# Attention tiles turned by TensorE in place of DMA, the last two score banks read by one exponential, and two units' bias moved from TensorE to a table

## The chip, the cores and the metric

The kernel runs on one core of one Trainium2 chip. The metric is the device time of one execution in microseconds. A core has five engines that each take their instructions in order and wait for one another through semaphores: TensorE (PE in the profile, its weight loads PEld), VectorE (DVE), ScalarE (ACT), GpSimd (POOL) and SyncE (SP). SP and POOL issue most of the DMAs.

## What is computed

Attention with a sliding window of 128 and a linear bias (ALiBi) for 8 batches of 8 heads, 576 positions and 64 dimensions; its output, seen as 4608 tokens of 512 features, goes through two matrix products with an ELU between them.

```python
scores = q @ k.T / sqrt(D)
mask = (rel >= 0) & (rel < 128)          # rel = query position - key position
scores = where(mask, scores - slope[head] * abs(rel), -1e9)
attn = softmax(scores)
x = (attn @ v).transpose(0, 2, 1, 3).reshape(4608, 512)
h = x @ w_in                             # w_in 512 x 2048
g = where(h > 0, h, exp(min(h, 0)) - 1)
out = g @ w_out                          # w_out 2048 x 512
```

## The kernel before

**Tiles.** Keys go in units u of 128 (u = 0 to 3; the last also takes the 64 keys left over). For each batch b and unit u the scores of all heads, keys on partitions, stand in four PSUM banks of 512 columns, `sp[0]` to `sp[3]`: two heads of 256 queries in each. `sp[0]` and `sp[1]` are the halves of one tile `spa`; `sp[2]` and `sp[3]` are tiles of their own. ScalarE takes the exponential into `EX[u]` (fp16), VectorE multiplies by a table `TAB` of exp(bias) with zeros outside the window, and a product with v, widened by a column of ones, gives a tile `xn` of 128 queries (64 in the fifth, i = 4) by 512 features, divided by that column's sum. The tile is turned, features to partitions, into a ring `xT`. From it come hidden blocks of 512 columns in the banks `hp[0]` and `hp[1]` by turns, then a relu or exponential on ScalarE, a second exponential on ScalarE or a minimum on GpSimd, and the ELU's end on VectorE (`g`). Output tiles of 256 tokens are formed by seven products of half-size matrices (Winograd's form of Strassen's scheme), `product`, from sums S1 to S4 of `g` and T1 to T4 of `w_out`.

**Batches 0 and 1.** They have functions of their own, since they run while the weights are still loading. For batch 0, units 0 and 1 in two calls each (`early_bias`, `early_scores`) and units 2 and 3 (`bias`, `first_scores`) put the bias into PSUM by a product of `SI` (identity times slope) with `RB` (distances, with a large negative number outside the window), and the scores are added to it. `RB` has 512 columns, the second 256 in the order of unit 3. Batch 1 is weighted by the table instead (`first_weigh`).

**Turning.** The nine tiles of batch 0 and of batch 1's first four are turned by TensorE (`turn_x`, L295: four transposes of 128 columns into a PSUM bank; L297: a copy to `xT` on ScalarE or VectorE). The other 31 tiles are turned by a DMA from SP's queue (`turn`, L287).

**Order.** The order is written out by hand in `SCRIPT`. Each token takes the next job from the queue of its name, and its instructions go to their engines in that order; a semaphore is waited for only where data or a buffer require it. The tokens that matter here:

- `f`, `fA`, `fD`: q and k of batches 0 and 1 turned by TensorE, and copied by ScalarE or VectorE; `b` bias; `i` scores of batches 0 and 1; `j` their exponentials; `W` `first_weigh`; `C` four copies that fill the second halves of `RB` and `TAB`
- `k` scores of a unit from batch 2 on (L222, 32 partitions an operand, four at a time); `x`, `y`, `z` exponentials of `spa`, `sp[2]`, `sp[3]` (L230, L233); `w` weighting of half a unit (L238)
- `v` product with v (L250, L271), `r` reciprocal, `n` division into `xn`; `T` the DMA transpose; `t`, then `tA` or `tD`: `turn_x` and its copy
- `h` a hidden block (L312), `p` and `q` its two steps to `e` (L319 to L325), `e` the ELU (L333)
- `oN` N steps of products (L403), one matmul of 256 columns each; `u` the copy of a finished product, `s1` to `s4` sums, `c1` to `c4` and `m` results and their stores; `O` outputs of the first 256 tokens
- `l` loads of `w_out`, q, k and v on POOL's queue; `d` q and k turned in blocks by VectorE

The first loads (k, q, v and the four quarters of `w_in`, L119) are issued by POOL ahead of `SCRIPT`.

Of the kernel before, what the change touches and what calls it, by code (L numbers as in the profile page):

```python
# [7 lines left out]
F32 = mybir.dt.float32  # L8
# [10 lines left out]
def kernel(  # L19
# [38 lines left out]
    RB = fore[3][:, 1024:1536]  # L58
# [18 lines left out]
    sp = [spa[:, 0, :], spa[:, 1, :]] + [ps_s.tile([128, 512], F32, name=f"sp{i}", tag=f"sp{i}") for i in (2, 3)]  # L77
# [72 lines left out]
    with tc.manual_schedule():  # L150
# [11 lines left out]
        def bias(u, half, d):  # L162
            r0 = 256 * int(u == 3)
            for x in (2 * half, 2 * half + 1):
                for hh in range(2):
                    c = 256 * (x % 2)
                    nc.tensor.matmul(pairs[d][hh][:, c:c + 256], SI[:, 4 * hh + x, :], RB[:, r0:r0 + 256],
                                     start=x % 2 == 0, stop=False, skip_group_check=True)

        def first_scores(b, u, half, d):  # L170

            heads = [(x, hh) for x in (2 * half, 2 * half + 1) for hh in range(2)]
            for o, kb, q0, n in blocks(u):
                for x, hh in heads:
                    r, c = slice(64 * hh, 64 * hh + 64), 256 * (x % 2) + o
                    k0 = x * S + 128 * kb
                    nc.tensor.matmul(pairs[d][hh][:, c:c + n], kt_[b][r, k0:k0 + 128], Q0[b][r, x, q0:q0 + n],
                                     start=b > 0, stop=True, skip_group_check=True)
# [48 lines left out]
        def expo(b, u, g):  # L227
            if g < 2:
                if g == 0:
                    nc.scalar.activation(unit(b, u)[:, 0:2, :, :], spa.rearrange("p g (h c) -> p g h c", h=2),  # L230
                                         AF.Exp, scale=0.125)
                return
            nc.scalar.activation(unit(b, u)[:, g, :, :], sp[g].rearrange("p (h c) -> p h c", h=2),  # L233
                                 AF.Exp, scale=0.125)
# [48 lines left out]
        def turn(b, i):  # L283
            n = 128 if i < 4 else 64
            o = (b * S + 128 * i) % RING
            x = xnt.pop((b, i)).rearrange("p g h d -> p (g h d)")
            nc.sync.dma_start_transpose(out=xT[:, :, o:o + n], in_=x[0:n, :])  # L287

        def turn_x(b, i, copy, bank):
            n = 128 if i < 4 else 64  # L290
            o = (b * S + 128 * i) % RING
            x = xnt.pop((b, i)).rearrange("p g h d -> p (g h d)")
            t = bank.bitcast(F16)[:, 0:512].rearrange("p (c r) -> p c r", c=4)
# [187 lines left out]
        V.scalar_tensor_tensor(out=RB[:, 0:256], in0=rel, scalar=-1.0, in1=far, op0=ALU.mult, op1=ALU.add)  # L481
# [5 lines left out]
        for h in range(H):  # L487
            nc.scalar.activation(TAB[:, 0, h // 2, h % 2, :], RB[:, 0:256], AF.Exp, scale=slope[h])
# [31 lines left out]
        for b in range(2, B):  # L520
# [19 lines left out]
            f fD f fD b f fA f fD C C C C b i j i j j b i j j v r n v r n b t tD v r n v r n  # L540
            h p q t tD f fA
            e h p q i j f fD f fA f fD b b i j i l
            h p q e j j l
            h p q e b i l
            h p q j v r n v r n e l
            h p q t tD b i j e l
            h p q e
            h p q e
            h p q e v r n v r n
            h p q e l O  # L550
            h p q e v r n t tA l
            h p q e a v r n l l l O
            h p q e a t tA
            h p q e a l O
            h p q e a l O O1 O2
            h p q e a l O
            h p q e a f fD f fA l l O
            h p q e a f fA f fD f fA f fA l l O
            e a l l s1 s3 O O1 O2 i j i j j
            W l l o7  # L560
            s2 W l l o1 u o6 v r n i j i j j
            l l o2 c1 o5 v r n
            W W d l o3 u o4 t tA i j v r n
            W l s4 o4 u o3 v r n
            h p q v r n i j d l
            h p q e W t tA d l o5 u o2
            h p q e v r n i j l
            h p q e W t tA l o7 c2
            h p q e v r n i j d l
            h p q e W l o7 u  # L570
            h p q e v r n v r n l c3 m s1
            o1 h o2 p o1 k l q o1 e o1 v y l t tA d o1
            h x r n e o1 T o1 p o4 s2 u
            h q w o2 e o2 z o4 d p o1
            h w q c1 o2 p v e o4 q o1 r
            h s3 u n o2 p o2 e o1 T o1 u k s4 q o1
            h x e d o2 p o3
            h w u q y l o1 z e o4 p o2 d o1
            h d q w l o1 e v p o2 c2 l o1 q o1
            h r n l o1 e o1 T p o2 l o2 s1 o1 q k l u o1 e o1 x  # L580
            h l d o2 p o1 s2 o4 u
            h w q y e o4 z o2 c3 o2 p o2 w m
            h q c1 v u e p o4 s3 o1 q o1
            h r n o2 p o1 e o1 T o1 k q s4 u
            h e x d o3 p o2 w o1
            h y q z l o1 e o1 u o3 p o1 w o2
            h q d l o1 v c2 p e o1 l o2 q o2 r o2 v l u e v o2
            h r l s1 n o2 p o2
            h r T n q n o2 p e k u d o1 q o3
            h x s2 e o2 p o3 w o3 q o1  # L590
            h c1 y e o1 z o2 s3 o2 p o3 w o1
            h u q c3 v m e T o3 u o2 r o1 p s4 o3
            h n q o1 e T o1 p k d u q
            h x l e o2 p o1 w o4 z o1 q
            h c2 y l e o2 p o2 w l o4 q
            h s1 l e o1 v l p o2 r o1 q l
            h n u d o2 p k e q o3 s2 o2 u
            h x e s3 o2 p o3
            h w q c1 y o1 e o4 z o2 c3 o2 p o1 s4
            h m T u w q o4 e v u p o2 r o3 n o1 q o1  # L600
            h T e o3 u k p c3 q
            h x l e o2 p o2 w o3 y o1 q
            h c2 z l e o2 p o2 w l o2
            h q s1 l v e p l o2 r o1 u v d q o1 m l o1
            h e o1 n o1 p o4 v r T q s2 o3
            h u e o1 s3 o1 p o2
            h r n q c1 o2 n p o3 e o1 T o2 q k d u
            h x e s4 o2 p o1
            h w z d q o5 u o2 e o1 p o4 y o2 q o1
            h u w o1 e o1 p o3 v c3  # L610
            h q r n l o2 e p o1 T o2 l o2 s3 q k l u c2
            h x e m l o3 p
            h w l q s1 l o2 z o2 e o3 y o5 p o1 w
            h q s2 v u e p o4 c1 o1 q
            h r n o2 e p o1 T o4 u s4 k q
            h x e d o2 p o3
            h w u q o1 y o1 e o4 p o2 d o1
            h z q u w l o2 p o3 e o2 v q
            h l r e o1 l n o1 p o5 s3 l T q k c2 u l e
            h x l o2 p o1 w o1  # L620
            h l q s1 o1 z o1 e o4 y o2 c3 o2 p
            h w m q s2 o1 v u p o1 v r o1 e o2 q o1 v c1 o3 e o1
            h u n o2 r p o1 T o1 n
            h r q n o2 T p e o3 k u s4 q
            h x e o2 d o1 p o4
            h z w q y e o2 u o2 p o2 w o4 q
            h c2 l e o2 p v l o2 r o2 s1 q o1
            h l u n o1 l o1 e p o1 T o2 k d l q o1
            h x e o2 p o1 w
            h u s2 q o3 z o1 e o4 y o2 c3 o1  # L630
            h p w m q c1 o1 v e o4 u o2 r o1 p
            h n q s3 T k p e o2 q o1 d o3
            h x e o1 s4 u o3 p
            h w z q o3 l u o1 e o2 p o4 y o1 c2 o1 q o1
            h w l v e p l o2 r o2 c3 o1 l o1 u
            h n q l s1 T m o2 p k e l q s3 o1
            h l x e l o1 s2 o1 p o5 d u o2 q o1
            h z e o1 y o2 w o2 p o2
            h w q c1 o2 e p v v q r o2 s4 o1
            h u e o2 n p v o3 r o1 q T o1 n o3 r o1 u o1 n o1  # L640
            h u e T d o1 k p o1 q x
            h e o2 p o1 w o4 y
            h q c2 z l e o2 p o3 w l o3 q
            h s1 l e o2 p v l o2 r o1 u
            h s2 q l n o2 p o2 c3 o3 u e o1 m T q k d
            h x e o2 p o1 w o1
            h q c1 o1 z o1 e o4 y o2 s3 o2 p
            h w q o2 v u e p o3 s4 o1 u o2
            h q r n o2 p o1 e o1 T o1 k q d
            h x e o2 u o1 w o1 p o5 y o1 q o3 z  # L650
            h e c3 o2 p
            h c2 w q o3 p v e u o2 r o1 q o1 m o1 n
            h s1 T o1 k p e u d q o3
            h x s2 e o2 p o4 c1 o1 z o2 s3 o1
            h q y e o3 p o2 w o2 u o2
            h q w e o2 p v s4 o1 u o1 v q r o2 r v
            h e n o2 p o2 r o1 T n o1
# [190 lines left out]
```

## Time and profile before

| | |
|---|---|
| Median of 3 runs | 304.71 us (304.34 to 305.03) |
| The profiled execution | 304.94 us, its span 303.2 us |
| Granted TensorE clock | 1.00 |
| Busy: TensorE, VectorE, ScalarE, GpSimd | 296.2, 256.2, 238.2, 109.1 us |
| First hidden block (L312) starts | 12.8 us |
| Hidden blocks, 256 columns (L312) | 768 matmuls, 99.6 us busy |
| Steps of products (L403) | 192 into op, 176 into av of the largest groups, 29.5 and 27.0 us busy |
| DMA transposes (L287) | 31 from 70.0 to 272.2 us, 2.3 / 3.1 / 8.8 us to landing (least, median, most) |
| Exponentials of scores (L230, L233) | 24 of 1024 columns at 1.02 us, 48 of 512 at 0.60 us |

How to read it: the span runs from the first to the last instruction. Busy times are unions of an engine's instructions; matmuls are pipelined, so one's duration (0.27 us for 256 columns) is longer than the time until the next one starts (0.109 us), and what a matmul costs is read from starts. A line like `PE hp L312 <- DMA xT<-xn: 0.4, 1, 0.4` says who waited for whom: in total, how often, and the longest, in us.

### The profile page before, as it was taken

The numbers are of one execution on the slowest core, as the hardware profiler recorded it, in microseconds if no ns is written. First come the engines' busy times: TensorE is split into PE (matmuls) and PEld (weight loads), VectorE is DVE, ScalarE is ACT, GpSimd is POOL, SyncE is SP. The second block draws the span as 40 slices with busy tenths as digits, with TensorE's granted clock in tenths as the row PEclk, the third lists the DMA queues.
The fourth block names the chain that finished last, engine by engine and source line by source line (L and its number), as shares of the span: only waits on it lengthen the run. The fifth ranks groups of instructions, "written<-read, shape, count | busy, mean of one in ns | idle before, by whom it ended". The sixth has DMA issues, their size and how long they took to land.

```text
span 303.2 us, 9837 instructions
## 1 busy us (share of the span) xinstructions
PE 296.2 (98%) x4074; PEld 255.6 (84%) x4074; DVE 256.2 (85%) x499; ACT 238.2 (79%) x445; POOL 109.1 (36%) x163
## 2 busy tenths in 40 slices
PE   7899999999999999999999999999999999999996
PEld 5688876989888889988888888887899888898885
DVE  5747879989999999799989898989989887885873
ACT  5577688869797888877979888888887888868881
POOL 8947958671534243332534162606000100010000
PEclk9999999999999999999999999999999999999999
DMA  8999999999394949491969695999220301111013
GB/s 99 193 198 201 201 178 192 125 128 101 36 160 72 131 78 119 83 184 21 161 60 130 107 118 66 130 144 125 61 89 2 97 17 54 54 56 43 37 57 118
DMA packets 96941, 32.04 MB, mean 106 GB/s; under 512 B 83968, under 2 KB 92800, under 8 KB 96896
## 3 DMA queue, kind: packets, MB, share of 16 engines
q0 software_dynamic: 75920, 18.36, 66.6%
q1 hardware_dynamic: 20832, 12.98, 18.0%
q8 instruction: 32, 0.52, 0.7%
q14 instruction: 13, 0.11, 0.1%
q10 hardware_dynamic: 144, 0.07, 0.1%
HBM read 36.70 MB, written 9.44 MB: 152 GB/s over the span
## 4 chain that ended last, share of the span: by engine, by line
PE 86%; DVE 4%; DMA 4%; ACT 2%; POOL 2%; issue 1%; POOLq 0%; DVEq 0%; ACTq 0%
PE hp L312 38%; PE op L403 15%; PE av L403 14%; PE spa L222 4%; PE spa L271 3%; DMA VP<-in_v_dram 2%; PE sp L403 2%; PE sp L312 2%; DMA xT<-xn 2%; PE sp L250 1%; DVE g L333 1%; PE op L339 1%; PE spa L339 1%; ACT e L323 1%; DVE xn L259 1%
## 5 line engine op out<-in xcount | busy, mean ns | idle before, releaser
L312 PE MATMUL hp<-xT,wi 128*128 128x256 f16 (+3 forms) x1488 | 144.1, 245 | 0.9 <-DMA xT<-xn 0.4
L312 PEld LDWEIGHTS <-wi 128*128 128x128 f16 x1600 | 120.6, 98 | 15.1 <-issue 3.9
L333 DVE SCALAR_TENSOR_TENSOR g<-e,hp 128x512 f16<-128x512 f32 x138 | 93.9, 681 | 23.4 <-ACT e L321 12.0
L325 POOL TENSOR_SCALAR e<-e 128x512 f32<-128x512 f32 x44 | 28.9, 657 | 151.4 <-ACT e L323 148.6
L319 ACT ACTIVATE e<-hp 128x512 f32<-128x512 f32 x98 | 58.7, 599 | 28.2 <-PE hp L312 22.9
L321 ACT ACTIVATE e<-e 128x512 f32<-128x512 f32 x100 | 63.6, 636 | 2.2
L403 PEld LDWEIGHTS <-S 128*128 128x128 f16 x544 | 51.0, 98 | 6.6 <-issue 1.1
L403 PEld LDWEIGHTS <-g 128*128 128x128 f16 x400 | 37.1, 98 | 5.4 <-issue 1.5
L238 DVE TENSOR_TENSOR EX<-EX,TAB 128x1024 f16<-128x1024 f16 x48 | 33.0, 694 | 2.8 <-ACT EX L233 1.3
L114 POOL DMA_DIRECT2D VP<-in_v_dram x40 | 34.4, 874 | 1.7 <-DMA s<-in_k_dram 1.3
L323 ACT ACTIVATE e<-hp 128x512 f32<-128x512 f32 x40 | 24.2, 605 | 12.1 <-PE hp L312 12.0
L403 PE MATMUL op<-T,S 128*128 128x256 f16 x192 | 29.5, 273 | 0.0
L403 PE MATMUL av<-T,S 128*128 128x256 f16 x176 | 27.0, 273 | 0.0
L233 ACT ACTIVATE EX<-sp 128x512 f16<-128x512 f32 x48 | 27.0, 602 | 0.0
L230 ACT ACTIVATE EX<-spa 128x1024 f16<-128x1024 f32 x24 | 24.5, 1022 | 1.0 <-PE spa L222 0.5
L364 DVE TENSOR_TENSOR S<-g 128x1024 f16<-128x1024 f16 (+2 forms) x35 | 23.1, 666 | 0.3 <-PE op L403 0.2
L403 PE MATMUL op<-wo,g 128*128 128x256 f16 x128 | 20.4, 273 | 0.0
L403 PE MATMUL av<-wo,g 128*128 128x256 f16 x120 | 19.7, 273 | 0.0
L108 POOL DMA_DIRECT2D st<-in_k_dram x24 | 16.3, 687 | 2.9 <-DMA s<-in_q_dram 2.0
L279 DVE TENSOR_TENSOR xn<-spa,rden 128x512 f16<-128x512 f32 x24 | 16.5, 687 | 0.4
L108 POOL DMA_DIRECT2D st<-in_q_dram x24 | 15.9, 666 | 1.3 <-DMA VP<-in_v_dram 1.3
L222 PE MATMUL spa<-QT,KT 32*128 32x256 f16 (+2 forms) x240 | 15.1, 250 | 0.0
(137 smaller groups left out, 381.5 us busy)
## 6 DMA issues: line engine op xcount, KB each, us to landing
out_dram<-ob SPq DMA_DIRECT2D x32, 256.0 KB, 3.2
VP<-in_v_dram POOLq DMA_DIRECT2D x32, 128.0 KB, 6.1
st<-in_k_dram POOLq DMA_DIRECT2D x24, 144.0 KB, 5.3
st<-in_q_dram POOLq DMA_DIRECT2D x24, 144.0 KB, 5.9
wi<-in_moe_w_in_dram POOLq DMA_DIRECT2D x4, 512.0 KB, 11.2
wo<-in_moe_w_out_dram POOLq DMA_DIRECT2D x4, 512.0 KB, 10.8
out_dram<-ob SPq DMA_DIRECT2D x7, 128.0 KB, 1.7
VP<-in_v_dram POOLq DMA_DIRECT2D x8, 64.0 KB, 6.1
```

Of the source, the lines that this page charges most:

```text
L108: nc.gpsimd.dma_start(st[b][32 * g:32 * g + 32, w, :, :, :, :].rearrange("p h n j d -> p (h n) (j d)"), (q, k)[w][b, 2 * g:2 * g + 2, :, : ...
L114: nc.gpsimd.dma_start(VP[b % 2][0:p, n, :, 0:D], v[b, :, 128 * n:128 * n + p, :].rearrange("h p d -> p h d"))
L222: nc.tensor.matmul(sp[g][:, 256 * h2 + o:256 * h2 + o + n], kt_[b % 2][r, k0:k0 + 255:2], qt_[b % 2][r, c0:c0 + 2 * n - 1:2], start=dh == ...
L233: nc.scalar.activation(unit(b, u)[:, g, :, :], sp[g].rearrange("p (h c) -> p h c", h=2), AF.Exp, scale=0.125)
L238: V.tensor_tensor(out=e, in0=e, in1=TAB[:, int(u == 3), 2 * gp:2 * gp + 2, :, :], op=ALU.mult)
L312: nc.tensor.matmul(p[:, l * w + u0:l * w + u1], w_in_sb[:, c, fc * 128:(fc + 1) * 128], xT[:, c, x0:x0 + u1 - u0], start=(c == 0), stop=(c ...
L319: nc.scalar.activation(e[:, 0:n], p[:, 0:n], AF.Relu, scale=-1.0)
L321: nc.scalar.activation(e[:, 0:n], e[:, 0:n], AF.Exp, scale=-1.0)
L323: nc.scalar.activation(e[:, 0:n], p[:, 0:n], AF.Exp)
L325: nc.gpsimd.tensor_scalar(out=e[:, 0:n], in0=e[:, 0:n], scalar1=1.0, scalar2=0.0, op0=ALU.min, op1=ALU.max)
L333: V.scalar_tensor_tensor(out=gs[t][:, f0:f0 + nf, c0:c0 + w], in0=sh(es.pop((t, c0, f0))), scalar=1.0, in1=sh(hps.pop((t, c0, f0))), op0=A ...
L403: nc.tensor.matmul(o, a[:, j, :], b[:, j, :], start=j == 0 and i in (1, 2, 5), stop=j == 7, skip_group_check=True)
```

## The change

`turn` goes; all 40 tiles are turned by `turn_x`, the 31 that were turned by DMA into bank `sp[3]`, with ScalarE copying. `sp[2]` and `sp[3]` become the halves of one tile `spb`, read by one exponential of 1024 columns, so `z` goes. `bias` goes: batch 0's units 2 and 3 start their scores afresh and are weighted by `first_weigh`; `RB` has 256 columns, and its two copies go. `SCRIPT` is laid out anew from the first line to the last.

```diff
-    RB = fore[3][:, 1024:1536]
+    RB = fore[3][:, 1024:1280]
...
-    sp = [spa[:, 0, :], spa[:, 1, :]] + [ps_s.tile([128, 512], F32, name=f"sp{i}", tag=f"sp{i}") for i in (2, 3)]
+    spb = ps_s.tile([128, 2, 512], F32, name="spb", tag="spb")
+    sp = [t[:, i, :] for t in (spa, spb) for i in range(2)]
...
-        def bias(u, half, d):
-            r0 = 256 * int(u == 3)
-            for x in (2 * half, 2 * half + 1):
-                for hh in range(2):
-                    c = 256 * (x % 2)
-                    nc.tensor.matmul(pairs[d][hh][:, c:c + 256], SI[:, 4 * hh + x, :], RB[:, r0:r0 + 256],
-                                     start=x % 2 == 0, stop=False, skip_group_check=True)
...
-                                     start=b > 0, stop=True, skip_group_check=True)
+                                     start=True, stop=True, skip_group_check=True)
...
-            if g < 2:
-                if g == 0:
-                    nc.scalar.activation(unit(b, u)[:, 0:2, :, :], spa.rearrange("p g (h c) -> p g h c", h=2),
-                                         AF.Exp, scale=0.125)
-                return
-            nc.scalar.activation(unit(b, u)[:, g, :, :], sp[g].rearrange("p (h c) -> p h c", h=2),
+            nc.scalar.activation(unit(b, u)[:, g:g + 2, :, :], (spa, spb)[g // 2].rearrange("p g (h c) -> p g h c", h=2),
                                  AF.Exp, scale=0.125)
...
-        def turn(b, i):
...
-            nc.sync.dma_start_transpose(out=xT[:, :, o:o + n], in_=x[0:n, :])
...
-        for f, *a in ((early_bias, AB, 0), (early_bias, sp[2:4], 128), (early_bias, (hp[1], av), 0), (early_bias, AB, 128),
-                      (bias, 2, 0, 0), (bias, 2, 1, 3), (bias, 3, 0, 0), (bias, 3, 1, 0)):
+        for f, *a in ((early_bias, AB, 0), (early_bias, sp[2:4], 128), (early_bias, (hp[1], av), 0), (early_bias, AB, 128)):
...
+        for u in (2, 3):
+            for half in range(2):
+                job("W", first_weigh, 0, u, half)
...
-            job("T", turn, b, i)
+            parts(turn_x(b, i, copies[0], sp[3]), "t", "tA")
...
-        for a in ((RB[:, 256:448], RB[:, 0:192]), (RB[:, 448:512], RB[:, 0:64]),
-                  (TAB[:, 1, :, :, 0:192], TAB[:, 0, :, :, 0:192]), (TAB[:, 1, :, :, 192:256], TAB[:, 0, :, :, 0:64])):
+        for a in ((TAB[:, 1, :, :, 0:192], TAB[:, 0, :, :, 0:192]), (TAB[:, 1, :, :, 192:256], TAB[:, 0, :, :, 0:64])):
...
-                for g, x in ((0, "x"), (2, "y"), (3, "z")):
+                for g, x in ((0, "x"), (2, "y")):
```

Counted by tokens, `SCRIPT` loses 31 `T`, 24 `z`, 4 `b` and 2 `C`, and gains 31 `t`, 31 `tA` and 4 `W`; all others are as many as before (896 single steps `o` among them). In matmuls, 16 go and 124 come: 4182 for 4074. Two of its new lines, from the middle:

```
h q u e t o2 tA s3 k p q
h n d o2 p t o1 e o2 tA k s4 q u
```

## The prediction

> **What bounds the kernel now.** I read the busy shares first, then the forty slices, the waits, the groups by form, and last the timeline at the places that the change touches.
>
> ```profile
> PE 296.2 (98%) x4074; PEld 255.6 (84%) x4074; DVE 256.2 (85%) x499; ACT 238.2 (79%) x445; POOL 109.1 (36%) x163
> ...
> PE   7899999999999999999999999999999999999996
> ...
> PE 86%; DVE 4%; DMA 4%; ACT 2%; POOL 2%; issue 1%; POOLq 0%; DVEq 0%; ACTq 0%
> ```
>
> TensorE is busy in 98% of the span, from the second slice on in nine tenths or more, and 86% of the chain that ended last is its own. A busy share can hide slow matmuls, so I took starts instead: 256 columns start every 0.109 us, 128 columns every 0.056 us. That is a dense stream. The waits say the same:
>
> ```profile
> PE op L448 <- DVE T L454: 1.2, 1, 1.2
> ...
> PE hp L312 <- DMA xT<-xn: 0.4, 1, 0.4
> ```
>
> After the first 12.8 us TensorE hardly stops. Of the 31 DMA transposes one was late, by 0.39 us (at 205 us), though half of them take more than 3.1 us to land. So every column that is added to TensorE after 12.8 us lengthens the span, unless it fills a hole, and work that is only taken off DMA, ScalarE or VectorE brings nearly nothing. From starts against the dense rate I find 8.0 us of holes after 12.8 us; 43 of them are of 0.096 us, where the stream goes over to operands of fewer partitions (each of the 24 score blocks has one), and these stay: 4.1 us. At most 3.9 us can be won by a better order.
>
> **The change part by part.**
>
> *Transposes.* 24 tiles of 128 rows and 7 of 64 (batch 1's last, then five a batch) go from SP's DMA queue to TensorE and ScalarE. The kernel already does this for nine tiles:
>
> ```profile
> 31.52 0.39 PE L295 MATMUL sp<-ident,xn 128*128 128x128 f16 x4
> 31.74 1.06 PE L312 MATMUL hp<-xT,wi 128*128 128x128 f16 x16
> ...
> 33.74 1.06 PE L312 MATMUL hp<-xT,wi 128*128 128x128 f16 x16
> 34.73 0.29 PE L295 MATMUL sp<-ident,xn 64*128 64x64 f16 x4
> 34.95 1.07 PE L312 MATMUL sp<-xT,wi 128*128 128x128 f16 x16
> ```
>
> From start to the next start a full tile costs 0.22 us. The 64-row tile costs 0.22 us too, and the block of 16 ahead of it took 0.99 us where 0.89 is the rule: its going over to 64 partitions costs another 0.10 us. Sum: 24 x 0.223 + 7 x 0.318 = 7.6 us, all on the path. A rule stands against that row. The Trainium skill, "TensorE: Matmul & The Clock Gate", Part 4: PE-mode transpose, has about 275 ns for a 128x128 transpose inside a kernel, and says that such work does not count as activity for the clock. By it 124 transposes cost 34 us. The row shows 56 ns each at a granted clock of 1.00, since their latency overlaps; I take the row. Another rule speaks for the change: "VectorE: DVE Perf Modes", Rules for kernel authors, wants 128x128 transposes on TensorE where PSUM will do; its table gives 390 ns against 1309 ns for the crossbar, which would be 124 x 0.92 = 114 us won if they stood in line. The trace has 0.39 us of waiting for them, so removal is worth 0.39 us. SP's stores no longer queue behind transposes that wait for xn; no engine waits for a store in the list of waits, so that is nothing.
>
> *Bias matmuls.* Four jobs of four, 256 columns each, go:
>
> ```profile
> 18.08 0.27 PE L167 MATMUL sp<-T 128*128 128x256 f16 x1
> 18.19 0.27 PE L167 MATMUL op<-T 128*128 128x256 f16 x1
> ...
> 25.45 1.07 PE L312 MATMUL hp<-xT,wi 128*128 128x128 f16 x16
> ```
>
> 16 x 0.109 = 1.74 us, all before 25.45 us. But the matmul at 25.45 is the seventh hidden block, the first to need the fourth quarter of w_in, and that DMA, issued at 12.34, landed at 24.58. The new order has the same blocks ahead of it, less the bias. So it can start 0.87 us earlier and no more: I take 0.87, with 1.74 as the other end. In exchange VectorE weighs four more halves, 4 x 0.684 = 2.7 us, less two small copies; it is busy 12.2 of the 20 us from 10 to 30. This lies beside the wait for w_in; without that cover, batch 0's third values would be late by about one weighing, 0.7 us.
>
> *Exponentials.*
>
> ```profile
> 87.44 1.08 ACT L233 ACTIVATE EX<-sp 128x512 f16<-128x512 f32 x2
> ...
> 203.03 1.02 ACT L230 ACTIVATE EX<-spa 128x1024 f16<-128x1024 f32 x1
> ```
>
> Two of 512 take 1.08 us one behind the other, one of 1024 takes 1.02. Merging 24 pairs takes 1.4 us off ScalarE (subtracting the mean durations, 2 x 602 - 1022, would claim 4.4 us; consecutive ones overlap). No weighing starts later for it, as it reads both banks. On the path: nothing.
>
> *ScalarE's new copies.* 24 x 0.58 + 7 x 0.35 = 16.4 us. 238.2 + 16.4 - 1.4 is 253 us, some 81% of the new span. Not a bound as a sum, but the copies bring the one new wait that I price.
>
> *The new wait.* x is turned in the fourth score bank, which the next score block overwrites. So scores (k) must wait until the copy (tA) has read it, and all later work on TensorE stands behind k. In the trace before none of the 24 score blocks waits: each begins 0.096 us late, the change of operands. How long does it take? The transposes at 31.52 have left TensorE's stream by 31.74; the copy began at 31.97 and took 0.58, so 0.81 us, and about 0.05 more until TensorE sees it (an xn that ended at 11.01 let weights load at 11.06). The first two score matmuls go to other banks with their 0.10 us of change, so about 0.76 us of other work is needed between t and k. Counting the single product steps (o, 0.109 us each) in the new order:
>
> ```
> t o2 tA s3 k                0.22 us
> t e o2 tA o3 c3 p t o2 tA o1 q k    0.33 us after the last t
> t o2 tA o1 u k              0.33 us
> t o1 e o2 tA k              0.33 us
> t p o1 s2 o3 tA o1 e k      0.55 us
> ```
>
> These five fall short by 0.54 + 3 x 0.43 + 0.21 = 2.0 us. Six more have 0.65 us, 0.1 short each (0.7 in all); the rest have enough. I take 2.0; the ends are 0 (the copy is seen sooner, or what I call filler is longer) and 3.5 (ScalarE still has an earlier exponential when the copy's turn comes). The other side of t is its wait for xn: from the end of values it takes 0.27 to the reciprocal, 0.20, 0.69 and 0.07, some 1.2 us, and the new order holds 1.1 to 1.5 us of TensorE work there in most tiles. I take nothing; VectorE, at nine tenths between 70 and 220 us, could make it 0.2 us in ten tiles, 2 us.
>
> *Sum.* 7.6 - 0.87 - 0.39 + 2.0 = 8.3 us on the span of 303.2. The profiled run took 304.94 us, 1.7 outside its span and 0.23 above the median of the runs, so I add the difference to the median 304.71: 313.0 us.
>
> **The rivals.**
>
> *A. The added columns alone.* No new wait, the whole bias won: 7.6 - 1.74 - 0.39 = 5.5, so 310.2 us. For it: the order before has no wait of scores at all, and a new order could have been laid out as well. Against it: the five counts above. With 1.5 us of the 3.9 us of holes closed, 308.7.
>
> *B. ScalarE's queue becomes late.* Between 70 and 220 us ScalarE is busy 84% and VectorE 91%. About half of 31 copies would each stand in front of a relu or exponential of the hidden blocks; TensorE alternates two hidden banks and its next block waits for the elu of the one before last. If 16 of them delay it by 0.25 us, 4 us come on top: 317 us. Against it: ScalarE itself waits 35 us for hidden banks (`e <- hp`), so it is mostly ahead.
>
> *C. The other side, faster.* One mechanism could do it: without transposes that land 2.3 to 8.8 us after issue, hidden blocks can be placed anywhere, and the order closes the holes in TensorE's stream after 12.8 us. It decides where the holes closed, the wait for DMA among them, pass 7.6 - 1.74 = 5.9 us. All that are not changes of operands are 3.9 us; with all closed, the full bias won and no wait of scores, 304.71 + 7.6 - 1.74 - 3.9 = 306.7, still slower. To get below, some 20 changes of operands must go as well, or two of the first 12.8 us, where the stream waits for DMA landings (v's second tile at 12.20) that the change does not touch: 304 us. I give it 4%.
>
> *D. The change does not do what it says* (transposes at the page's 275 ns, or the clock lost): 339 us. The nine tiles there speak against it; 1%.
>
> **How the numbers follow.** My sum with its ends (311.0 to 315.5) 55%, A 22%, B 16%, C 4%, D 1%, and 2% for no change within 0.2%. About 0.2% (0.6 us) is what a measurement of this kernel can tell from no change. Range: from A with closed holes, 308.7, to B with a little over, 317.5. Faster 4%, same 2%, slower 94%.
>
> **What would show it.** Right: 124 more transposes with 0.056 us between starts, in sp's place; TensorE's share of the span still 97% or more; no DMA_TRANSPOSE; waits of scores on ScalarE's copy of xT of 0.2 to 0.5 us at about five of the 24 blocks; the seventh hidden block starting near 24.6 us on w_in; ScalarE near 253 us. Wrong: transposes at 0.1 us or more each, score blocks that begin without a wait (then A), waits of hidden blocks on elu summing to microseconds (then B), a first hidden block well before 12.8 us (then C).

## The result, and the profile after

The changed kernel takes 321.13 us (median of 4 runs, 320.43 to 321.99) against 304.65 us for the kernel before: the ratio is 1.0542, with an interval of 1.0511 to 1.0573. That is 16.5 us more, where 8.3 were forecast: the direction was right, the time lies above the range (308.7 to 317.5). The profiled execution took 320.43 us with a span of 318.6, which is 15.5 more than the span before; the traces can place these 15.5.

The page after, the same rows as before (engines, TensorE's slices, the chain that ended last):

```profile
PE 306.1 (96%) x4182; PEld 261.3 (82%) x4182; DVE 260.4 (82%) x501; ACT 249.7 (78%) x452; POOL 109.4 (34%) x163
...
PE   7878999999999999999999999999999999999995
...
PE 78%; DVE 7%; ACT 5%; POOL 3%; DMA 2%; issue 2%; POOLq 0%; DVEq 0%; ACTq 0%
```

TensorE's share of the span fell from 98% to 96%, and its own share of the chain from 86% to 78%; what the chain gained is VectorE, ScalarE and GpSimd. So TensorE is not only given more work, it waits more. From starts against the dense rate (each matmul's start to the next one's start, less what it takes in a dense stream), the holes after 12.8 us grew by 9.8 us, from 8.0 to 17.8. The work added at the dense rate is 31 x 0.22 - 1.74 = 5.1 us; together that makes 14.9 of the 15.5 us.

TensorE's waits up to 60 us, first of the kernel before, then after (what waits, whose result it waits for: us in total, times, longest):

```profile
PE op L448 <- DVE T L454: 1.2, 1, 1.2
PE hp L295 <- DVE xn L259: 0.5, 2, 0.3
PE hp L136 <- DMA s<-in_q_dram: 0.4, 1, 0.4
PE av L250 <- DMA VP<-in_v_dram: 0.4, 1, 0.4
```

```profile
...
PE spa L170 <- DVE QT L142: 1.1, 1, 1.1
PE spb L385 <- DVE xn L247: 0.9, 2, 0.5
PE spb L277 <- DVE xn L247: 0.6, 2, 0.3
PE hp L294 <- DVE xT L279: 0.5, 1, 0.5
...
PE spb L137 <- DVE g L315: 0.5, 1, 0.5
PE spa L185 <- DVE KT L142: 0.4, 1, 0.4
```

None of these six is in the list before, and all six wait for VectorE. Two of them, the products of L385 and the turns of q and k of L137, hang on the new joint tile `spb`: with separate banks (`a_split` below) they are gone. The transposes of L277 wait for the x that they turn; with separate banks they wait just as long:

```profile
PE sp L281 <- DVE xn L251: 0.6, 2, 0.3
```

All this is in the first 60 us, where the prediction had a gain of 0.87 us.

To place the loss I took the start of each of the 144 hidden blocks as a ruler. The 19th, where the steady part begins, starts at 54.32 us before and 57.51 after: 3.2 us are lost by then. From there to the 144th 11.4 us are added, of which transposes of x 6.9, score blocks 2.4, products 1.4, other 0.7 (starts to starts, by kind; 0.4 of the products are four that stood in the head or at the end before). After it come 0.9 more. The prediction put 7.6 + 2.0 - 0.39 = 9.2 us into the steady part and a gain of 0.87 into the head. With the moved products put back, it is short by some 2 us in the steady part, 1 at the end and 4 in the head: the head of the kernel is the place of the largest error.

The timeline of TensorE, then of ScalarE, where scores stand close behind a turn, in the changed kernel (start us, us, engine, line, operation, tiles, form, count, wait):

```profile
193.80 0.39 PE L277 MATMUL spb<-ident,xn 128*128 128x128 f16 x4
194.02 0.38 PE L385 MATMUL op<-T,S 128*128 128x256 f16 x2
194.24 0.27 PE L385 MATMUL av<-T,S 128*128 128x256 f16 x1
194.45 0.29 PE L215 MATMUL spa<-QT,KT 32*128 32x256 f16 x2
194.91 0.29 PE L215 MATMUL spb<-QT,KT 32*128 32x256 f16 x2 [0.17 <-ACT xT L279]
```

```profile
194.28 0.58 ACT L279 COPY xT<-spb 128x512 f16<-128x512 f16 x1
```

The transposes take 0.22 us of the stream (193.80 to 194.02), as in the tiles of before. The copy ends at 194.86, and the third score matmul, the first into `spb`, starts at 194.91. From the transposes' end that is 0.89 us, 0.43 of it filled by products: the wait that was priced, at one of the five places that were counted out.

### The profile page after: what moved, and what is told of

It reads as the page before. It is cut to its first block, busy times and chain, and to the rows that moved or that the text cites. A ratio compares the mean times of both kernels' runs of the same rounds, so it can differ in the third digit from the quotient of the medians.

```text
span 318.6 us, 9968 instructions
## 1 busy us (share of the span) xinstructions
PE 306.1 (96%) x4182; PEld 261.3 (82%) x4182; DVE 260.4 (82%) x501; ACT 249.7 (78%) x452; POOL 109.4 (34%) x163
## 4 chain that ended last, share of the span: by engine, by line
PE 78%; DVE 7%; ACT 5%; POOL 3%; DMA 2%; issue 2%; POOLq 0%; DVEq 0%; ACTq 0%
PE hp L294 34%; PE op L385 14%; PE av L385 13%; DVE g L315 3%; PE spa L259 3%; PE spa L215 3%; PE spb L277 2%; DMA VP<-in_v_dram 2%; PE spb L385 2%; PE spb L215 2%; POOL e L307 2%; ACT e L305 1%; DVE xn L247 1%; PE spb L238 1%; ACT e L301 1%
## 5 line engine op out<-in xcount | busy, mean ns | idle before, releaser
L315 DVE SCALAR_TENSOR_TENSOR g<-e,hp 128x512 f16<-128x512 f32 x138 | 93.9, 681 | 32.5 <-ACT e L303 15.7
L385 PEld LDWEIGHTS <-S 128*128 128x128 f16 x544 | 50.4, 98 | 7.3 <-issue 2.0
L385 PEld LDWEIGHTS <-g 128*128 128x128 f16 x400 | 37.1, 98 | 5.2 <-issue 1.3
L385 PE MATMUL op<-T,S 128*128 128x256 f16 x192 | 30.3, 273 | 0.0
L385 PE MATMUL av<-T,S 128*128 128x256 f16 x176 | 27.6, 273 | 0.0
L221 ACT ACTIVATE EX<-spb 128x1024 f16<-128x1024 f32 x24 | 24.4, 1016 | 0.0
L279 ACT COPY xT<-spb 128x512 f16<-128x512 f16 (+1 forms) x34 | 18.2, 534 | 6.2 <-PE spb L277 5.8
L385 PE MATMUL op<-wo,g 128*128 128x256 f16 x128 | 20.9, 273 | 0.0
L385 PE MATMUL av<-wo,g 128*128 128x256 f16 x120 | 18.3, 273 | 0.0
L267 DVE TENSOR_TENSOR xn<-spa,rden 128x512 f16<-128x512 f32 x24 | 16.5, 689 | 0.7
```

Source lines behind the costliest of these rows:

```text
L221: nc.scalar.activation(unit(b, u)[:, g:g + 2, :, :], (spa, spb)[g // 2].rearrange("p g (h c) -> p g h c", h=2), AF.Exp, scale=0.125)
L315: V.scalar_tensor_tensor(out=gs[t][:, f0:f0 + nf, c0:c0 + w], in0=sh(es.pop((t, c0, f0))), scalar=1.0, in1=sh(hps.pop((t, c0, f0))), op0=A ...
L385: nc.tensor.matmul(o, a[:, j, :], b[:, j, :], start=j == 0 and i in (1, 2, 5), stop=j == 7, skip_group_check=True)
```

## Experiments

**What a part of the change costs inside the changed kernel.** My first theory: turning costs about 10 us with its waits (T3 in the texts below), and the joint tile `spb`, which makes users of two unrelated banks wait for one another, the rest (T1). The rival: the new order of the instructions costs it (T2). In `a_split` the banks are apart again, in `a_dma` the 31 turns go through the DMA again (`turn_d` issues the transpose at `t` and does nothing at `tA`), `a_split_dma` has both.

```diff
 a_split
-    spb = ps_s.tile([128, 2, 512], F32, name="spb", tag="spb")
-    sp = [t[:, i, :] for t in (spa, spb) for i in range(2)]
+    sp = [spa[:, 0, :], spa[:, 1, :]] + [ps_s.tile([128, 512], F32, name=f"sp{i}", tag=f"sp{i}") for i in (2, 3)]
...
+                for i in (2, 3):
+                    nc.scalar.activation(unit(b, u)[:, i, :, :], sp[i].rearrange("p (h c) -> p h c", h=2),
+                                         AF.Exp, scale=0.125)
 a_dma
-            parts(turn_x(b, i, copies[0], sp[3]), "t", "tA")
+            parts(turn_d(b, i), "t", "tA")
```

> The changed kernel with one part undone: sp[2] and sp[3] are tiles of their own again, each with its own exponential (both issued where the joint one stood). All else, order included, as changed. Theory T1 (the joint tile makes unrelated uses of its two banks wait for one another, most of all before 58 us): 321.1 - 4 = 317 us, the 19th hidden block at some 54 us in place of 57.5, and no wait of a product in sp[3] for xn read from sp[2]. Theory T2 (the new order and the four extra weighings cost the early time, whatever the tiles are): 321 us, the 19th hidden block still at 57.5. ScalarE 1.4 us more busy in both.

> The changed kernel with one part undone: the 31 tiles are turned by DMA from SP's queue again, issued where the transposes stood; nothing is copied by ScalarE for them. Theory T3 (transposes cost their columns and the score blocks' wait for the copy, no more): 7.6 + 2.4 us less, 311 us; score blocks at 0.57 us each; the 19th hidden block still at 57.5 us. Rival: the copies also hold up ScalarE and with it the hidden blocks, then 3 us more are won, 308 us. Other rival: hidden blocks now wait for late DMA landings in an order made for early ones, then 313 us or more, with waits of hidden blocks on DMA.

> The changed kernel with both parts undone: separate tiles and DMA transposes; left are the new order and the table in place of batch 0's bias. T1 and T3 together: 321.1 - 10 - 4 = 307 us or less, down to 304 if the new order is as good as the old. T2: 311 us, the early loss still there.

Measured: `a_split` 320.05 us, ratio 1.0479 [1.0440, 1.0517]; `a_dma` 313.63, 1.0264 [1.0234, 1.0294]; `a_split_dma` 312.16, 1.0224 [1.0189, 1.0259]. The joint tile and its exponential are worth 0.4% (`a_dma` to `a_split_dma`) to 0.6% (changed kernel to `a_split`), 1.2 to 1.9 us (a difference of two such ratios is known to about 0.4%). Turning is worth 2.8% or 2.6%, 8.5 or 7.8 us. What stays with both undone, the order and the table, is 2.24%, 6.8 us. My first theory falls: its 304 to 307 us for `a_split_dma` is missed by 5 at least, and 317 for `a_split` by 3; the rival's 311 is off by 1. From TensorE's waits of `a_split_dma`, first up to 60 us, then behind it:

```profile
...
PE spa L169 <- DVE QT L141: 1.1, 1, 1.1
PE hp L306 <- DVE xT L291: 0.6, 1, 0.6
...
PE spa L184 <- DVE KT L141: 0.4, 1, 0.4
```

```profile
PE hp L306 <- DVE g L327: 1.4, 5, 0.3
```

With separate banks and no turns, the waits for VectorE's copies of q and k and for x^T are still there in the head, and later five hidden blocks wait for the ELU that frees their bank. In the kernel before, the only wait listed after 60 us was the DMA's 0.4. The largest of the waits of `a_split_dma` shown here, 1.1 us for q, is not the order's: it comes with the table, in the old order too (`b_table`, next). The waits for k, for x^T and for the ELU are not in the list of `b_table`, but for one of 0.16 us; they come with the order.

`a_dma` shows one thing more. Its 24 score blocks take 14.5 us from start to start, where the kernel before has 13.6 and the changed one 16.0, though nothing is copied out of a score bank in the steady part. Three blocks make up these 0.9 us, and behind two of them a hidden block waits for its ELU:

```profile
217.07 0.49 PE L302 MATMUL hp<-xT,wi 128*128 128x256 f16 x3 [0.30 <-DVE g L323]
...
232.98 0.44 PE L302 MATMUL hp<-xT,wi 128*128 128x128 f16 x5 [0.31 <-DVE g L323]
```

In the changed kernel scores wait for the copy at two of these three places, 0.46 and 0.40 us, and no wait for the ELU is listed behind them. So 2.4 us are lost at the score blocks, but only 1.5 of them go when turning goes.

**The order and the table, taken apart.** `b_table` is the kernel before, in its own order, with the table in place of the bias. On top of it, `h_newhead` takes the new order up to the 19th hidden block, `h_newtail` from there on; in both the turns stay with the DMA and the banks apart. `b_table2` is `b_table` with one hidden block moved into the hole that the bias left.

```diff
 b_table (jobs and the table as in the changed kernel; SCRIPT of before without four b, with four W)
-            e h p q i j f fD f fA f fD b b i j i l
+            e h p q i j f fD f fA f fD i j i l
 b_table2
-            e h p q i j f fD f fA f fD i j i l
-            h p q e W j j l
+            e h p q i j f fD f fA f fD h i j i l
+            p q e W j j l
```

> The kernel before with one part of the change alone: batch 0's units 2 and 3 are weighted by the table, the four bias jobs and the two copies of RB go, and the four weighings stand in the old order behind the elu of the next line or two. As the prediction had it (bounded by the landing of w_in's fourth quarter): 0.9 us faster, 303.8 us, the seventh hidden block at 24.6 us in place of 25.45. T2: the weighings hold up VectorE's queue and batch 0's values, 305.5 us or more.

> The kernel b_table (old order, separate banks, DMA transposes, table) with its order taken from the changed kernel up to the 19th hidden block, and from there the old order of what is left. The new order with separate banks and DMA transposes took 312.2 us beside 305.2, b_table 305.3. Theory T4a (half of these 7 us is lost in the first 58 us, to waits for VectorE's copies, xn and weighings): 308.7 us, the 19th hidden block some 2.5 us later than in b_table. Rival (all of it is lost here): 312 us; (none of it): 305.3 us.

> The kernel b_table with the old order up to the 19th hidden block and the changed kernel's order from there on. Theory T4b (half of the 7 us is lost after 58 us, in waits of hidden blocks and score blocks for VectorE's elu and weighing): 308.7 us. Rivals: 312 us if all of it is lost there, 305.3 us if none.

> The kernel before with the bias of units 2 and 3 replaced by the table (as in b_table, 305.3 us beside 305.2), and the third hidden block moved from behind to ahead of the scores of unit 2. Theory T5 (in b_table TensorE waited 1.1 us there for VectorE's copy of Q, a wait that the bias matmuls had filled, and this ate what their going won): the hidden block fills it, 0.9 us faster than before, 304.3 us, no wait of L177 for QT. Rival (the loss only moves on, to the copy's next reader or to the landing of w_in): 305.2 us.

Measured: `b_table` 305.29 us, 1.0006 [0.9986, 1.0026]: in the old order, taking 1.74 us (0.57%) of matmuls away gives nothing that can be seen. `h_newhead` 307.91, 1.0095 [1.0065, 1.0126]; `h_newtail` 309.46, 1.0140 [1.0109, 1.0172]. The two halves add up to 2.35%, against 2.24% for order and table in `a_split_dma`. Over `b_table` it is 0.9% for the head and 1.3% for the steady part and the end. `b_table2` 305.76, 1.0039 [1.0022, 1.0056]: my way to get the bias's time back failed. One line each from the waits of `b_table`, `b_table2` and (behind 58 us) `h_newtail`:

```profile
PE spa L177 <- DVE QT L141: 1.1, 1, 1.1
```

```profile
PE hp L312 <- DVE g L333: 1.1, 3, 0.7
```

```profile
PE hp L312 <- DVE g L333: 1.5, 5, 0.4
```

In the kernel before, the bias of unit 2 ran while VectorE copied q: the matmuls were filler. Without them TensorE waits 1.1 us for that copy. With a hidden block as filler the wait for q is gone, but hidden blocks then wait 1.1 us for the ELU, where 0.2 was listed before. In the steady part of the new order, five hidden blocks wait for the ELU of the block before the last, 1.5 us, where `b_table` has one of 0.16. By starts, the holes of `h_newtail` between the 19th and the 144th hidden block exceed those of `b_table` by 4.2 us; about 3 of them stand right ahead of a hidden block, 0.7 within the products with v.

**The joint tile in the old order.** `b_merge` has the joint tile and the joint exponential alone, `b_tie` the joint tile with the two exponentials as before.

```diff
 b_merge and b_tie
-    sp = [spa[:, 0, :], spa[:, 1, :]] + [ps_s.tile([128, 512], F32, name=f"sp{i}", tag=f"sp{i}") for i in (2, 3)]
+    spb = ps_s.tile([128, 2, 512], F32, name="spb", tag="spb")
+    sp = [t[:, i, :] for t in (spa, spb) for i in range(2)]
 b_merge alone: one activation of spb at y, every z taken out of SCRIPT
```

> The kernel before with one part of the change alone: sp[2] and sp[3] as one tile, read by one exponential where that of sp[2] stood; order, bias and DMA transposes as before. Theory T1 in its smaller form (the joint tile makes unrelated uses of its two banks wait for one another; 1.1 to 1.6 us in the new order): 306.7 us, with waits of TensorE in sp[3] for reads of sp[2] before 65 us. The prediction's account (nothing on the path): 305.2 us.

> The kernel before with its third and fourth score bank in one tile, the exponentials still apart. T1 (what costs is that the tile is one: every reader of one bank holds up every writer of the other, whatever reads it): about the 315 us of the joint tile with the joint exponential, 312 to 316. Rival (what costs is the joint exponential, which starts only when all four heads' scores are there and frees both banks together): 305 to 307.

Measured: `b_merge` 315.40 us, 1.0346 [1.0317, 1.0375]; `b_tie` 313.33, 1.0238 [1.0189, 1.0288]. I had expected at most 306.7 of the first. TensorE's waits of `b_tie`:

```profile
PE spb L313 <- ACT xT L298: 1.4, 1, 1.4
PE spb L137 <- ACT KT L142: 1.3, 1, 1.3
...
PE spb L251 <- DVE g L334: 1.0, 1, 1.0
...
PE spb L251 <- ACT U L411: 0.7, 1, 0.7
PE spb L404 <- DVE ob L365: 0.6, 1, 0.6
PE spb L404 <- DVE xn L260: 0.6, 1, 0.6
```

These are hidden blocks, turns of k, values and products that write one of the two banks and wait for an ELU, a copy or a result that is read from the other. In the kernel before, where each bank is a tile of its own, none of these six waits is listed. `b_tie` differs from it in nothing but the tile, so in this kernel a wait is set for the tile, not for the bank that is used. Most of the loss lies in the head: by the 19th hidden block `b_tie` is 6.9 us late (0.3 of it was there at the first block), 0.6 more comes by the 144th and 0.8 behind it. The joint exponential, which can't begin until all four heads' scores are there, adds 1.1% by the two ratios, known to some 0.6%; by the ruler `b_merge` loses 2.2 us between those blocks, 1.6 more than `b_tie`.

So the same tile costs 10.5 us in the old order and 1.2 to 1.9 in the new. The waits of the new order that hang on the joint tile (`spb` L385, L137 and one of L277 for the ELU) come to 1.7 us, the six above to 5.6: I take it that the new order moved the users of the two banks apart.

**Turning in the old order.** `b_turn` puts `t` and `tA` where `T` stood, a few of them put off until the bank had been taken over; `b_turn2` puts two more off; `b_turn3` leaves all where they stood and moves the reciprocal or exponential that reads the bank ahead of six of them. In all three, five turns (the fourth tile of batches 2 to 6) still overwrite bank `sp[3]` before the attention values in it have been divided, and in `b_turn` two more overwrite scores, so some columns of x differ from the reference's; the count and the size of the instructions do not. What their expectations say on this does not hold, and `b_turn_klate` further down has the same fault as `b_turn`.

```diff
 SCRIPT, b_turn3 (one of 31 places)
-            h r n o2 p o1 e o1 T o1 k q s4 u
+            h r n o2 p o1 e o1 t tA o1 k q s4 u
```

> The kernel before with its own order, separate banks and the bias as it was; the 31 turns through the DMA are replaced, where they stand in the order, by TensorE's transposes and ScalarE's copy (4 of them put off by a few instructions, until the bank is read). T1 (transposes cost their own time, and the score block that follows waits for the copy as far as the work between is under 0.76 us): transposes 7.6 us; the order leaves 0 to 0.55 us of work between, mean about 0.2, so 21 waits of about 0.55, some 11 us: 304.7 + 7.6 + 11, about 323. Rival (the scheduler's order doesn't matter to the waits, the wait is the 2.4 us in all of the changed kernel): about 314.5.

> The kernel before with the 31 turns by TensorE and ScalarE in its own order, each placed where its bank is free (6 put off by a few instructions), so that all is computed as in the reference. T1 (transposes 7.6 us, and the score blocks wait some 10 us for the copies, since the old order leaves 0.2 us of work between): the same as the earlier kernel with turns in the old order, ratio 1.066 to 1.075. Rival (two transposes that overwrote a score bank caused part of the wait): under 1.06.

> The kernel before with the 31 turns by TensorE and ScalarE exactly where the DMA turns stood; where a bank was not yet read there, its reader (6 of them) is moved ahead of the transposes. T1 (7.6 us of transposes and some 10 us of waits of score blocks for the copy out of the bank): ratio 1.066 to 1.078, as with the turns put off. Rival (turns that stood behind their hidden block, or a score bank overwritten, made part of that time): under 1.06.

Measured: 327.58 us, 1.0708 [1.0653, 1.0763]; 328.83, 1.0780 [1.0750, 1.0809]; 328.20, 1.0753 [1.0719, 1.0786]. So turning costs about 23 us in the old order, so far as these three can say it, and 8 in the new. In `b_turn3` the transposes take 8.0 us between the 19th and the 144th hidden block (starts to starts; 7.6 was the prediction's term), and the score blocks 23.7 us in place of 13.6. That is 18 of the 22.3 us lost there. From its waits behind 58 us:

```profile
PE sp L222 <- ACT xT L297: 4.3, 13, 0.5
PE sp L295 <- ACT EX L233: 1.8, 2, 1.0
```

Thirteen score matmuls are listed as waiting for the copy out of `sp[3]`. From starts, the score blocks as a whole take 10.1 us more, near the 11 that the formula of the prediction gives: the old order leaves 0 to 0.55 us between `t` and `k` where 0.76 is needed. The second line is the two turns ahead of which an exponential was moved.

**Scores further behind the turn.** If scores wait for the copy, one could move them behind the next hidden block. `b_turn_klate` does that to 21 score blocks of `b_turn`, `a_split_klate` to 11 of `a_split`.

```diff
 SCRIPT, a_split_klate (one of 11 places)
-            h n e t p o3 s4 o2 tA o1 k u q
-            h x e d o2 p o5 w o1 q o3
+            h n e t p o3 s4 o2 tA o1 u q
+            h k x e d o2 p o5 w o1 q o3
```

> As the kernel with the turns by TensorE in the order of before, and each score block that stood less than 0.75 us behind its transposes moved behind the next hidden block (21 of them), which puts 0.87 us of work between. T1: only the transposes' own 7.6 us stay: 312 to 313. Rival (the exponentials start later and the values' product waits for them): 314 to 317.

> The changed kernel with its two banks separate and the exponentials apart, and with 11 score blocks that stood under 0.75 us behind their transposes moved behind the next hidden block. T1 (these blocks wait for the copy, 2.4 us in all): about 2 us under the kernel with separate banks alone (ratio 1.048), so 1.042. Rival (the wait is only moved on, to the exponential's readers): 1.047 to 1.050.

Measured: `b_turn_klate` 332.36 to 338.03 us, 1.0903 [1.0817, 1.0988]; `a_split_klate` 326.67, 1.0682 [1.0619, 1.0745], where `a_split` had 1.0479. Both theories of mine missed, and the rivals too; moving the scores made each kernel slower by 2%, where the second was to be faster by 0.6%. VectorE's waits for the first exponential, in `a_split` and in `a_split_klate`:

```profile
DVE EX L230 <- ACT EX L221: 2.2, 4, 1.1
```

```profile
DVE EX L230 <- ACT EX L221: 4.9, 8, 1.1
```

And TensorE's waits for the ELU behind 60 us, in the same order:

```profile
PE hp L298 <- DVE g L319: 0.8, 3, 0.3
```

```profile
PE hp L298 <- DVE g L319: 4.6, 13, 0.8
```

The score blocks themselves do begin sooner after their turn (13.8 us in all, 15.7 in `a_split`). But the exponential is late and VectorE stands at the weighing that needs it, 2.7 us more in the lines above. The ELU stands behind the weighing in VectorE's order, and the hidden block that needs the ELU's bank waits. The 2 us saved at the scores are lost at the hidden blocks, and more: 3.8 us in the waits listed here.

**The bias in the new order.** `a_bias` and `a_bias2` are one kernel: the changed one with the 16 bias multiplications and the two copies of `RB` back, each four multiplications ahead of their scores. `a_bias2` and `after_again`, the changed kernel itself, ran on one chip.

```diff
...
+                      (bias, 2, 0, 0), (bias, 2, 1, 3), (bias, 3, 0, 0), (bias, 3, 1, 0)):
...
-        for u in (2, 3):
-            for half in range(2):
-                job("W", first_weigh, 0, u, half)
 SCRIPT: b put ahead of the fifth to the eighth i, the first four W taken out, two C put in
```

> The changed kernel with the bias of batch 0's third and fourth unit added by TensorE again (16 multiplications of 256 columns, each four right ahead of the scores they belong to) and without the table's weighing of these units. T1 (TensorE waits for the query's copy there anyway, 1.1 us, and for other late work, so the multiplications fill a hole): no difference from the changed kernel, ratio to before 1.052 to 1.056. Rival (the 16 multiplications lie on the path, as the prediction took it, 0.87 to 1.74 us): 1.057 to 1.060.

> The changed kernel once more, beside the one with the bias put back, on one chip: ratio to before as measured, 1.051 to 1.057.

> The changed kernel with the 16 bias multiplications put back, beside the changed kernel on the same chip. T1 (they fill a wait): within 0.15% of the changed kernel. Rival (they lie on the path, the prediction's 0.87 us): 0.28% over it; all on the path with nothing waited less: 0.57% over it.

Measured: `a_bias` 322.55 us, 1.0568 [1.0539, 1.0596]; `after_again` 320.79, 1.0513 [1.0486, 1.0541]; `a_bias2` 322.35, 1.0560 [1.0532, 1.0588]. On one chip the bias costs 0.47%, 1.4 us; from the two intervals the difference is known to about 0.39%, so this is more than nothing, and both the 0.87 us that the prediction took and its other end, 1.74, lie within. Against the first runs of the changed kernel it is 0.2%. My theory of filler, which held for the wait for q in the old order, is not borne out in the new one. With the bias back, the wait at the scores of unit 2 is no longer for q:

```profile
PE spa L168 <- ACT EX L199: 0.6, 1, 0.6
```

## Why the prediction missed

**The step that failed: the new order, a term of zero.** The sum went over the edits one by one. It took the rewritten `SCRIPT` as neutral where no turn was concerned ("the same blocks ahead of it, less the bias"), and otherwise only as something to win by ("at most 3.9 us can be won by a better order"); that an order can also cost stood in no term. With turns and banks undone, the order and the table together cost 6.8 us (`a_split_dma`), where the sum had a gain of 0.87. Step by step from the changed kernel the 16.5 us are:

| undone | us | in the sum |
|---|---|---|
| the 31 turns (`a_dma`) | 8.5 | 7.6 + 2.0 - 0.39 = 9.2 |
| the joint tile and its exponential, too (`a_split_dma`) | 1.2 | 0 |
| what is left, the order and the table | 6.8 | -0.87 |

So the last row is 7.7 of the 8.2 us that were missed. If the table gives some 1.4 us back in this order, the order by itself costs about 8; that figure is a difference of two comparisons and was not run alone.

**What the order may be for.** In the old order turning costs 23 us and the joint tile 10.5, in the new one 8 and 1.5. If the two simply add in the old order, which was not run, the change without the new order would stand near 338 us. So the new order spares much of what the change would cost; whether its own 8 us are the price of that, no run shows.

**Mis-sized: "Merging ... On the path: nothing".** It looked at ScalarE's time and at the weighing, and not at what a joint tile ties together. It costs 1.2 to 1.9 us here, and 10.5 in the order of before.

**Right: the transposes.** 7.6 us was the term. In the steady part of the changed kernel the turns took 6.9 us from start to start, and going over to 64 rows is counted in the work ahead of them; in `b_turn3` it is 8.0. Each full tile is 0.22 us at a granted clock of 0.999 in the changed kernel. Rival D, transposes at 275 ns each, is not what these runs show.

**Right in kind, near in size by luck: the wait of scores for the copy.** 2.0 was the term, 2.4 was measured, but not where it was counted. The five places that were priced at 2.0 lost 1.3. At three of them the tile has 64 rows and its copy takes 0.37 us, not the 0.58 that the count used. The six that were called 0.1 short each, and left out, lost 0.8 (0.35 of it at one, where ScalarE still had a relu to do when the copy's turn came), the other blocks the rest. And 0.9 of the 2.4 is lost at the same blocks without any turn (`a_dma`). The need of 0.76 us of other work between `t` and `k` also gave the 10 us of the old order (11 was expected). The upper end of the sum, 315.5, asks that nothing be won by the bias; with the ends as they are listed it would be 314.5.

**Not settled: the bias.** 0.87 was taken, about 1.4 measured, known to within 1.2 us. The reason given was wrong: the seventh hidden block starts at 25.85 us and not near 24.6, and is not held by the landing of the last quarter of `w_in` (24.08); TensorE had lost its time to the copies of k and q (0.45 and 1.06 us) and to xn (0.6) before.

**The rivals.** B (317 us by waits of hidden blocks for their ELU) did not happen in the changed kernel as told: 0.7 us in three such waits is listed. ScalarE is busy 249.7 us, near the 253 that were forecast, and is not the bound. A counted the bias whole, but no wait of scores, and there were some. C, the holes closing, went the other way: the holes grew by 9.8 us. Of the signs named, two failed: the seventh hidden block near 24.6 us, and TensorE's share of 97% or more. The second points at the cause, TensorE standing still.

**What stays open.** The 6.8 us of order and table are placed (head 0.9% of the time, the rest 1.3%) and the largest waits in them are named, but no run shows which of the moved instructions make them. No version ran faster than the kernel before; `b_table` and the kernel before can't be told apart.

## What to carry to other kernels

When a change rewrites the order of a dense stream, price the order as a part of its own: go through the waits that the old order has not got, and ask at each new neighbour what it waits for, above all in the start-up, where work that looks superfluous may be filling a wait. Before joining two buffers to save an instruction, list everyone who writes or reads either: from then on each waits for the other's users. And work that stands between a producer and its reader can't be put there for nothing; moving the reader back made its own readers late, here for more than the wait had cost.

## What the runs showed beyond that

The start of the first hidden block differs from run to run of the same kernel by more than 1 us: 14.10 us in `a_bias`, 12.43 in `a_bias2` (12.54 in the changed kernel, 12.93 when it ran again). In `a_bias` 1.4 us of it is a wait for v's DMA. So a gain of half a microsecond in the first 13 us can't be read from one trace.

Tying two PSUM banks to one tile, without any new instruction, cost 2.4% of the time (`b_tie`).
